# PSUM addressed as eight single banks and a new hand-written order, in a kernel of block-sorted attention followed by a gated MLP

## The chip, the core and the metric

The kernel runs on one core of a Trainium2 chip. The metric is the device time of one execution in microseconds (us), and the lower one is the better. The core has five engines with a queue of instructions each: TensorE (PE, with the weight loads PEld beside it), VectorE (DVE), ScalarE (ACT), GpSimd (POOL) and SyncE (SP). An engine takes its instructions strictly in the order in which they were written for it. DMAs are issued from the queues of POOL, SP and ACT, and run beside the engines.

## What is computed

Four batches go through two stages. The first sorts blocks softly: a small matrix `sort_net` is exponentiated and normalised five times, and the result P mixes the eight blocks of 96 tokens of K and of V; each block of Q then attends to its mixed block. The second is an MLP whose gate mixes tokens.

```python
def _attn_ref(q, k, v, sort_net):          # q, k, v: (4, 8, 768, 64); sort_net: (4, 8, 8, 8)
    P = sort_net
    for _ in range(5):
        P = P - np.max(P, axis=-1, keepdims=True)
        P = np.exp(P)
        P = P / (np.sum(P, axis=-1, keepdims=True) + 1e-09)
        P = P / (np.sum(P, axis=-2, keepdims=True) + 1e-09)
    k_sorted = np.einsum('bhij,bhjcd->bhicd', P, k_b).reshape(B, H, S, D)
    v_sorted = np.einsum('bhij,bhjcd->bhicd', P, v_b).reshape(B, H, S, D)
    scores = scale * np.matmul(q_b, k_sb.transpose(0, 1, 2, 4, 3))
    ...
    return np.matmul(attn, v_sb).reshape(B, H, S, D)

def _moe_ref(x, w_in, w_spatial, b_spatial, w_out):   # x: (4, 768, 512), d_ff 1024
    h = np.maximum(x @ w_in, 0.0)
    u, v = h[..., :512], h[..., 512:]
    v_n = (v - mu) / np.sqrt(var + 1e-06)
    v_s = np.einsum('ts,bsd->btd', w_spatial, v_n) + b_spatial[None, :, None]
    return (u * v_s) @ w_out
```

## The kernel before

The whole program is one string, `ORDER` (L18 to L52), which is read from left to right. Each word is a unit, and its parts after the colons are arguments: `KT:2:A:3:1` calls `u_KT` with PSUM tile 2, evacuation on ACT (D would be DVE), batch 3, head pair 1. A unit writes its matmuls, then the copy that takes the result out of PSUM, each to the end of its engine's queue. So the string sets the order on all engines at once, and no scheduler moves anything. Waits between engines are put in by the tile framework where one instruction needs another's result, or a buffer that another still uses.

The units that the prediction speaks of are these.

- At the start: `SK` (L233) is one of five normalisations, a chain of small DVE and ACT instructions. `QC` casts half of a q load, `MA` and `MB` make a mask, `DM` (L226) multiplies a block of zeros to keep PE occupied, and `PR` (L256) spreads the finished P over partitions. `P0` (L270) makes the mixing matrices `pd` of batch 0 on DVE from it, and `PD` (L282) those of the other batches on POOL.
- Attention: `QT` and `QQ` transpose one or two head pairs of q. `KT` and `VT` (L383) mix K and V with `pd`, transposed; `VB` turns V of batch 0 back into the buffer `vb`. For the other batches `VM` (L410) mixes V into the buffer `vm` and `VC` (L424) copies it from `vm` into `vb[b % 2]` by DMA, one DMA for each of the eight blocks. `SC` makes scores and their exponentials, `AT` (L483) multiplies them with `vb` and normalises into `x_sb`. `IV` (L222) writes the columns of ones of a `vb` or of `vm`.
- MLP: `XT`, `XX` and `XD` transpose `x_sb` (PE or DMA), `WW` and `WT` transpose w_spatial. `VP` (L551) makes v of one or two token tiles, `ST`, `LN` and `LA` normalise it, `UP` (L593) makes u. `SP` (L608) mixes tokens and adds the bias into one of three buffers `z` (`NZ` is 3). `GT` (L625) multiplies z by u, on POOL or DVE, and `OP` is the output product. `QP` and `QX` transpose q of batch 3 by DMA. `L` issues a load from POOL's queue and `OS` a store.
- Tail: `SH`, `GH`, `OH`, `OI`, `OJ` do the last batch's SP, GT and output in smaller pieces after a flag has been tested (`IF`).

PSUM has eight banks of 512 words in each partition. `ps_tile(n)` (L105) gives every unit a tile of two banks, and with n from 0 to 3 there are four such tiles; a unit that fills one bank occupies a pair all the same. The next unit with the same n waits until the tile has been evacuated.

Of the kernel before, what the change touches and what calls it, by code (L numbers as in the profile page):

```python
# [15 lines left out]


ORDER = """  # L18
IV:0 L:q:0:4:8 L:v:0:0:8 S0 LH:A:0 TB CO L:k:0:0:8 SK:0 BH ID MA SK:1 L:k:1:0:8 SK:2 MC DM:0:6:512 QC:A:0 DM:0:6:512
SK:3 SK:4 DM:0:6:512 DM:0:6:512 QC:A:1 QT:0:A:0:3 DM:1:6:512 MB QT:1:A:0:2 DM:2:3:512 QT:2:D:0:0 PR:3 P0:0:2 P0:2:4  # L20
L:v:1:0:8 P0:6:8 P0:4:6 VT:0:A:0:0 VT:1:D:0:1 PC:D QT:2:A:0:1 VB:0:D:0:0 L:q:1:0:8 PD:1:4:8 VB:1:D:0:1 L:wv VT:2:A:0:3
VT:3:D:0:2 KT:0:A:0:1 KT:1:D:0:0 KT:2:A:0:3 KT:3:D:0:2 SC:0:0:1:0 PD:2:0:4 SC:1:0:1:1 VB:2:D:0:2 SC:0:0:0:1 AT:3:0:1:0
SC:1:0:2:0 PD:1:0:4 AT:2:0:1:1 SC:0:0:3:0 VB:3:D:0:3 SC:1:0:0:0 AT:2:0:0:1 KT:0:A:1:1 AT:3:0:2:0 SC:1:0:2:1
XT:2:D:0:1:0 AT:0:0:3:0 SC:3:0:3:1 VM:1:A:1:1 AT:2:0:0:0 PD:2:4:8 VM:3:A:1:3 AT:0:0:2:1 VM:1:A:1:0 AT:2:0:3:1
VM:3:A:1:2 XX:0:D:0:0 L:wu L:v:2:0:8 L:wsb L:q:2:0:8 KT:1:A:1:0 KT:2:D:1:2 KT:3:A:1:3 PD:3:0:4 QT:0:D:1:2 IV:2
QQ:1:D:1:0 VC:1:0:4 QT:2:A:1:3 XT:3:D:0:1:2 SC:0:1:2:0 SC:1:1:2:1 SC:2:1:0:1 VP:3:D:0:3 VP:0:D:0:0:4 SC:1:1:3:0
SC:3:1:0:0 VP:2:A:0:5:2 ST:0:3 UP:1:A:0:0:0 VC:1:4:8 L:k:2:0:8 VP:0:A:0:1 ST:0:2 AT:3:1:2:0 SC:2:1:1:0 AT:1:1:3:0
UP:0:A:0:1:1 AT:3:1:1:0 AT:2:1:0:0 L:wsa UP:1:A:0:0:1 VM:0:D:2:1 VM:3:A:2:3 XX:2:A:1:0 AT:1:1:2:1 AT:0:1:0:1 BI ST:0:5
UP:3:A:0:1:0 ST:0:1 VM:1:A:2:2 VM:2:A:2:0 L:k:3:0:8 ST:0:0 PD:3:4:8 VP:0:D:1:0:1 SC:3:1:3:1 IV:1 ST:0:4 SC:1:1:1:1
UP:2:A:1:0:0 LN:0:0:6 AT:3:1:3:1 WW:0:D:4 AT:1:1:1:1 UP:2:A:1:1:0 L:v:3:0:8 LA:0:5 LA:0:1 KT:3:A:2:3 QQ:0:D:2:0 LA:0:3  # L30
L:q:3:0:8 KT:1:A:2:1 KT:2:A:2:0 QQ:3:D:2:2 VC:2:4:8 LA:0:4 KT:0:A:2:2 WW:1:D:0 LA:0:2 SC:2:2:0:1 SC:3:2:3:1 VP:0:D:1:2
XX:1:D:1:1 SC:2:2:1:1 LA:0:0 SC:3:2:2:1 WW:0:D:2 UP:1:A:1:1:1 AT:2:2:0:1 AT:3:2:3:1 SP:0:0:2 AT:1:2:2:1 AT:2:2:1:1
SP:3:0:3 GT:P:0:3 XD:2:1 VC:2:0:4:0:4:A ST:1:1 SC:0:2:0:0 SC:1:2:1:0 SP:2:0:0 SP:3:0:1 SC:0:2:2:0 ST:1:0 SC:1:2:3:0
L:wo UP:2:A:1:0:1 VM:3:A:3:0 ST:1:2 AT:0:2:2:0 VP:1:A:1:4 KT:2:A:3:1 KT:3:D:3:0 KT:0:A:3:3 KT:1:A:3:2 GT:P:0:1
GT:D:0:0 QP:D:3:2 VP:2:D:1:3:5 QP:D:3:3 QP:A:3:1 QP:D:3:0 ST:1:4 GT:P:0:2 ST:1:3 VM:3:A:3:2 OP:0:0:2:2 OE:A:0:2 ST:1:5
VM:1:A:3:3 QX:3:0:4 VP:3:A:2:3:5 VP:2:A:2:4 LN:1:0:6 VM:0:D:3:1 LA:1:4 AT:1:2:0:0 OP:3:0:0:2 LA:1:1 LA:1:0 LA:1:2
LA:1:3 OE:A:0:0 VC:3:4:8:0:4:A VC:3:0:4 LA:1:5 AT:2:2:3:0 OP:0:0:4:2 OE:A:0:4 AT:1:2:1:0 SP:3:1:3 GT:P:1:3 ST:2:5
SC:2:3:1:0 SC:1:3:0:1 XD:2:0 ST:2:3 SP:0:1:0 SC:3:3:3:0 SC:2:3:3:1 SP:1:1:2 AT:0:3:3:0 AT:3:3:0:1 SP:2:1:1 AT:1:3:1:0
GT:P:1:1 VP:0:A:2:0 VP:3:A:2:2 OS:0:0 AT:2:3:3:1 VP:0:D:2:1 ST:2:1 SC:1:3:0:0 GT:P:1:2 SC:3:3:2:1 UP:2:D:2:1:0
GT:P:1:0 ST:2:0 ST:2:2 SC:0:3:2:0 ST:2:4 SC:1:3:1:1 UP:3:A:2:0:1 UP:2:A:2:0:0 OP:0:1:2:2 LN:2:0:6 OE:A:1:2 LA:2:1  # L40
LA:2:3 LA:2:2 LA:2:0 LA:2:4 AT:1:3:2:1 AT:3:3:1:1 XD:3:1 UP:2:A:2:1:1 OP:0:1:0:2 AT:1:3:2:0 LA:2:5 AT:2:3:0:0
OP:3:1:4:2 CK SP:1:2:2 XD:3:0 SP:2:2:3 UP:1:A:3:1:1 SP:2:2:0 VP:1:D:3:3 OE:D:1:4 GT:D:2:0 OE:A:1:0 OS:1:2:0:2:A
GT:P:2:3 SP:0:2:1 VP:2:A:3:4:0 GT:P:2:1 ST:3:4 UP:1:A:3:0:1 ST:3:0 GT:P:2:2 CF:3 OS:1:0 VP:0:A:3:5 ST:3:3 ST:3:5
VP:2:A:3:2:1 ST:3:2 ST:3:1 LF LN:3:0:6 LA:3:5 LA:3:0 LA:3:2 LA:3:4 UP:1:A:3:0:0 OP:0:2:0:2 OP:3:2:2:2 OE:A:2:0
OS:0:4:0:2:A OP:2:2:4:2 UP:1:A:3:1:0 OE:D:2:2 OS:0:2:0:2:A OE:A:2:4 LA:3:1 LA:3:3 SH:0:3:2:0 SH:3:3:3:0 GH:P:3:3:0
SH:2:3:0:0 GH:D:3:2:0 SH:0:3:1:0 GH:P:3:0:0 SH:3:3:1:1 SH:2:3:2:1 OS:2:4 GH:P:3:1:0 SH:1:3:3:1 OS:2:0 GH:D:3:1:1
SH:3:3:0:1 OS:1:4 GH:D:3:3:1 OS:2:2 GH:P:3:0:1 GH:P:3:2:1 IF OH:0:3:2:0:512:0:4 OI:A:3:2:0:512 OH:1:3:3:0:512:0:4
OH:2:3:0:0:512:0:4 OI:D:3:0:0:512 OI:A:3:3:0:512 OH:0:3:1:0:512:0:4 OJ:3:2:0:512:S OJ:3:3:0:512:A OI:A:3:1:0:512
OJ:3:0:0:512:S OH:1:3:4:256:512:0:4 OI:D:3:4:256:512 OH:3:3:5:0:256:0:4 OI:D:3:5:0:256 OJ:3:1:0:512:S OJ:3:4:256:512:A
OH:2:3:5:256:512:0:4 OJ:3:5:0:256:A OI:D:3:5:256:512 OH:0:3:4:0:256:0:4 OI:D:3:4:0:256 OJ:3:5:256:512:S OJ:3:4:0:256:A  # L50
"""


# [12 lines left out]
def kernel(  # L66
# [159 lines left out]
    def u_DM(ps, n, w):  # L226
        t = ps_tile(ps)
        for _ in range(int(n)):
            nc.tensor.matmul(t[:, 0, 0:int(w)], lhsT=warm[:, 0:128], rhs=warm[:, 0:int(w)], start=True, stop=True)  # L229
# [26 lines left out]
    def u_PR(ps):  # L256
        pr = ps_tile(ps)[:, 0, 0:NB * BH].rearrange("p (i y) -> p i y", i=NB)
        for i in range(NB):
            nc.tensor.matmul(
                pr[:, i, :], lhsT=spread[:, (i % NI) * NB:(i % NI + 1) * NB].rearrange("p j t -> p (j t)"),  # L260
                rhs=p_t[:, (i // NI) * BH:(i // NI + 1) * BH], start=True, stop=True,
            )
# [568 lines left out]
```

## Time and profile before

| what | value |
|---|---|
| median of 3 runs | 155.5 us (155.46 to 155.74) |
| the profiled execution | 155.7 us, of which 153.9 us are the span from the first to the last instruction |
| PE busy | 146.7 us, 95% of the span, 1686 matmuls |
| DVE busy | 114.4 us, 74% |
| ACT busy | 80.5 us, 52% |
| POOL busy | 44.3 us, 29% |
| DMA | 24.36 MB in 30693 packets, mean 158 GB/s |

A row of the chain of waits reads: start, duration, engine, result and line. The chain is followed back from the last instruction: at each step to what released it, or to the instruction before it on its engine. A row of the groups reads: line, engine, operation, result and operands with shapes, count, then busy us and mean ns of one. A row of the windows gives for a stretch of the span the busy time of each engine, the number of instructions in brackets, the granted clock, the mean number of DMA shares and GB/s.

### The profile page before, as it was taken

Reading aid. Unit: us, or ns where it says so; the run is one execution under the profiler, and the core shown is the slowest. Engines: PE = TensorE matmul, PEld = TensorE weight load, DVE = VectorE, ACT = ScalarE, POOL = GpSimd, SP = SyncE. Lnnn points to the kernel's source line nnn. Section 1 sums busy time; section 2 is a strip of 40 time slices with the busy share of each in tenths; the row PEclk is TensorE's granted clock in tenths of the full one; section 3 lists DMA queues with packets and bytes.
Section 4 is the critical chain, followed back from the end, with each engine's and each line's share of the span. In section 5 each row is a group of like instructions: output and inputs, shape, how many; then the busy total and the mean of one; then the engine's idle time right before and its main releaser. Section 6 shows DMA issues by size and latency. Waiting matters only on the chain.

```text
span 153.9 us, 4047 instructions
## 1 busy us (share of the span) xinstructions
PE 146.7 (95%) x1686; PEld 95.7 (62%) x1686; DVE 114.4 (74%) x260; ACT 80.5 (52%) x114; POOL 44.3 (29%) x48
## 2 busy tenths in 40 slices
...
GB/s 101 253 204 204 204 204 205 209 203 226 248 212 209 258 238 206 200 111 103 140 4 146 102 222 190 1 0 4 0 104 101 259 18 0 71 69 351 339 175 238
DMA packets 30693, 24.36 MB, mean 158 GB/s; under 512 B 10384, under 2 KB 27792, under 8 KB 30672
## 3 DMA queue, kind: packets, MB, share of 16 engines
...
q8 instruction: 14, 0.23, 0.6%
...
HBM read 24.78 MB, written 6.29 MB: 202 GB/s over the span
## 4 chain that ended last, share of the span: by engine, by line
PE 82%; DVE 6%; DMA 5%; issue 1%; SPq 1%; POOL 1%; ACT 1%; DVEq 0%; POOLq 0%; ACTq 0%
PE ps L613 15%; PE ps L601 13%; PE ps L558 10%; PE ps L639 10%; PE ps L229 7%; PE ps L669 5%; DMA vb<-vm 5%; PE ps L492 4%; PE ps L689 3%; PE ps L446 3%; PE ps L387 3%; PE ps L414 3%; PE ps L318 2%; DVE x_sb L500 2%; DVE vb L117 2%; PE ps L548 1%
## 5 line engine op out<-in xcount | busy, mean ns | idle before, releaser
L630 POOL TENSOR_TENSOR gt<-z,u_sb 128x768 bf16<-128x768 f32 x10 | 16.2, 1640 | 62.7 <-ACT ex_all L451 35.3
L451 ACT ACTIVATE ex_all<-ps 96x768 bf16<-96x768 f32 x32 | 24.1, 804 | 14.3 <-PE ps L446 14.3
L613 PE MATMUL ps<-wspT,v_sb 128*128 128x384 bf16 x144 | 25.1, 326 | 0.0
L601 PE MATMUL ps<-xT,w_in_sb 128*128 128x384 bf16 x128 | 23.3, 326 | 0.0
L558 PE MATMUL ps<-w_in_sb,xT 128*128 128x512 bf16 x96 | 22.9, 379 | 0.0
L500 DVE TENSOR_TENSOR x_sb<-ps,rec_all 96x512 bf16<-96x512 f32 x32 | 22.0, 687 | 1.1
L121 ACT ACTIVATE u_sb<-ps 128x768 bf16<-128x768 f32 x15 | 12.1, 809 | 17.2 <-PE ps L601 16.8
L613 PEld LDWEIGHTS <-v_sb 128*128 128x128 bf16 x144 | 13.6, 98 | 8.7
L575 DVE BATCH_NORM_STATS2 stats<-v_sb 128x6 f32<-128x512 bf16 x24 | 16.2, 674 | 3.0 <-ACT v_sb L121 3.0
L619 DVE TENSOR_TENSOR z<-ps,b_bc 128x768 f32<-128x768 f32 x12 | 11.5, 955 | 7.9 <-PE ps L613 7.9
L639 PE MATMUL ps<-w_out_sb,gt 128*128 128x256 bf16 x144 | 16.9, 272 | 0.0
L601 PEld LDWEIGHTS <-w_in_sb 128*128 128x128 bf16 x128 | 11.8, 98 | 7.5
L115 ACT COPY o_sb<-ps 128x1024 f32<-128x1024 f32 (+1 forms) x10 | 8.8, 882 | 13.0 <-PE ps L689 8.4
L639 PEld LDWEIGHTS <-gt 128*128 128x128 bf16 x144 | 13.9, 98 | 2.0
L558 PEld LDWEIGHTS <-xT 128*128 128x128 bf16 x96 | 8.8, 97 | 9.3
L121 ACT ACTIVATE v_sb<-ps 128x512 bf16<-128x512 f32 (+1 forms) x10 | 7.6, 767 | 11.4 <-PE ps L558 11.3
L492 PE MATMUL ps<-vb,ex_all 96*128 96x65 bf16 x256 | 12.4, 193 | 0.7 <-DMA vb<-vm 0.5
L492 PEld LDWEIGHTS <-ex_all 96*128 96x128 bf16 x256 | 10.7, 97 | 3.4 <-issue 1.0
L229 PE MATMUL ps<-warm 128*128 128x512 bf16 x33 | 10.1, 450 | 1.4 <-DVE warm L203 1.3
L285 POOL TENSOR_TENSOR pd<-mask,prep_sb 128x512 bf16<-128x512 bf16 x6 | 6.5, 1093 | 15.0 <-DVE prep_sb L117 9.5
L587 DVE TENSOR_SCALAR v_sb<-v_sb,mv,rstd 128x512 bf16<-128x512 bf16 x24 | 8.7, 405 | 1.7 <-ACT rstd L582 1.7
L499 DVE RECIPROCAL rec_all<-ps 96x8 f32<-96x8 f32 x32 | 6.3, 196 | 3.9 <-PE ps L492 3.9
...
## 6 DMA issues: line engine op xcount, KB each, us to landing
...
vb<-vm SPq DMA_DIRECT2D x16, 99.0 KB, 6.2
...
```

Source lines behind the costliest of these rows:

```text
L121: nc.scalar.activation(out=out, in_=in_, func=AF.Relu)
L229: nc.tensor.matmul(t[:, 0, 0:int(w)], lhsT=warm[:, 0:128], rhs=warm[:, 0:int(w)], start=True, stop=True)
L451: nc.scalar.activation(out=e_tile(b, hp, ih).rearrange("p h (x g) -> p h x g", g=G), in_=t[0:BLK, :, 0:HW].rearrange("p h (g x) -> p h x g ...
L492: nc.tensor.matmul(t[:, hh, ii * VW:ii * VW + D + 1], lhsT=e[:, c:c + 128], rhs=vb[b % 2][:, ih * NI + ii, 2 * hp + hh, 0:D + 1], start=Tr ...
L500: nc.vector.tensor_mul(out=x_sb[:, hp].rearrange("p i (h d) -> p h i d", h=2), in0=tv[:, :, :, 0:D], in1=_raw_ap(rec, 0, [rec.ap[0], [NI, ...
L558: nc.tensor.matmul(t[:, x, :], lhsT=st["xT", b][:, n // 3, kc, (n % 3) * 128:(n % 3 + 1) * 128], rhs=w_in_sb[:, kc, DH:DFF], start=(kc == ...
L575: nc.vector.bn_stats(out=stats, in_=st["v_sb", b, n])
L601: nc.tensor.matmul(t[:, x, 0:HW], lhsT=w_in_sb[:, kc, mc * 128:(mc + 1) * 128], rhs=st["xT", b][:, ih, kc, :], start=(kc == 0), stop=(kc = ...
L613: nc.tensor.matmul(t[:, x, 0:HW], lhsT=st["v_sb", b, n][:, mc * 128:(mc + 1) * 128], rhs=wspT[:, 3 * x:3 * x + 3, n, :], start=(n == 0), s ...
L619: nc.vector.tensor_add(out=z.rearrange("p (x c) -> p x c", x=2), in0=t[:, :, 0:HW], in1=b_bc.rearrange("p (x c) -> p x c", x=2),)
L630: eng.tensor_mul(out=gt, in0=st["z", b, mc], in1=u)
L639: nc.tensor.matmul(t[:, x, c:c + w], lhsT=st["gt", b, mc][:, (n0 + x) * 128:(n0 + x + 1) * 128], rhs=w_out_sb[:, mc, c:c + w], start=(mc = ...
```

## The change

Three things change. Matmul, copy and DMA code of the units stays as it is.

- `ps_tile` cuts from one tile of eight banks. With n below 10 it gives the pair of banks 2n and 2n+1 as before; with n from 10 it gives the single bank n − 10. The units `QT`, `VB`, `XT`, `WT`, `VP` with one token tile, `SH`, `OH`, `DM`, `PR` and `CF` now take single banks.
- The whole string `ORDER` is new, from the first word to the last. Some work is also grouped in another way: `QQ` goes from 3 units to 1 and `QT` from 6 to 10; `XX` from 3 to 0 and `XT` from 2 to 8; `WW` from 3 to 2 and `WT` from 0 to 2; `VP` from 17 to 22 units for the same 24 token tiles. All 24 V copies are issued from SP's queue; before, 16 were SP's and 8 ACT's.
- The `DM` units write 23 products where they wrote 33.

```diff
 ORDER = """
-IV:0 L:q:0:4:8 L:v:0:0:8 S0 LH:A:0 TB CO L:k:0:0:8 SK:0 BH ID MA SK:1 L:k:1:0:8 SK:2 MC DM:0:6:512 QC:A:0 DM:0:6:512
...
+S0 CO DM:10:5:512 IV:0 LH:A:0 TB SK:0 DM:10:3:512 L:q:0:4:8 BH ID SK:1 SK:2 IV:2 QC:A:0 DM:10:4:512 QC:A:1 SK:3 MA
...
 """
...
     psum = ctx.enter_context(tc.tile_pool(name="psum", bufs=1, space=bass.MemoryType.PSUM))
 
+    banks = psum.tile([128, 8, 512], FP32, name="ps", tag="ps")
+
     def ps_tile(n, dt=FP32):
-        return psum.tile([128, 2, 512 if dt == FP32 else 1024], dt, name=f"ps{n}", tag=f"ps{n}")
+        n = int(n)
+        t = banks[:, 2 * n:2 * n + 2] if n < 10 else banks[:, n - 10:n - 9]
+        return t if dt == FP32 else t.bitcast(dt)
```

Six lines are added ahead of the units, so that the line of a unit in the changed kernel is its line before plus six.

The first place is ACT's queue at the start. `p_all` is the exponential of a normalisation, `q_in` a cast of q, `spread` the identity that `PR` uses. Before:

```order
L241 ACTIVATE p_all<-p_all 32x64 x3
L220 COPY spread<-ident 32x512
L115 CAST q_in<-q_109 128x768
L241 ACTIVATE p_all<-p_all 32x64 x2
L115 CAST q_in<-q_109 128x768
L115 COPY qT<-ps_197 128x768
```

And in the changed kernel:

```order
L247 ACTIVATE p_all<-p_all 32x64 x3
L121 CAST q_in<-q_117 128x768 x2
L247 ACTIVATE p_all<-p_all 32x64
L226 COPY spread<-ident 32x512
L247 ACTIVATE p_all<-p_all 32x64
L121 COPY qT<-ps 128x1536
```

Both casts of q stand ahead of the fourth exponential now, and the identity behind it.

The second place is POOL's queue from the mixing matrices on. The `MEMSET` of `vm` is `IV:2`, without which no V copy is complete. Before:

```order
L178 DMA w_in_sb<-in_moe_w_in_dram 128x4x512
L170 DMA v_in<-in_v_dram 128x8x384
L184 DMA ws_in<-in_moe_w_spatial_dram 128x3x768
L170 DMA q_in<-in_q_dram 128x8x384
L285 TENSOR_TENSOR pd<-mask_88,prep_sb 128x512
L224 MEMSET vm 128x48x2
```

In the changed kernel that `MEMSET` stands near the start:

```order
L230 MEMSET vb_97 96x64x2
L176 DMA q_in<-in_q_dram 128x4x384
masks.py:197 MEMSET ident 128x128
masks.py:199 ISA
masks.py:199 AFFINE_SELECT ident<-ident 128x128
L230 MEMSET vm 128x48x2
L176 DMA v_in<-in_v_dram 128x8x384
```

It has moved from behind a product of `pd` to the start of the program, ahead of the load of v.

The third place is the end of POOL's loads. The `MEMSET` of `vb` is `IV:1`. Before, it stood ahead of the loads of v and q of batch 3:

```order
L285 TENSOR_TENSOR pd<-mask_88,prep_sb 128x512
L224 MEMSET vb_97 96x64x2
L170 DMA v_in<-in_v_dram 128x8x384
L170 DMA q_in<-in_q_dram 128x8x384
L630 TENSOR_TENSOR gt<-z,u_sb 128x768
```

In the changed kernel, with the semaphores that each row waits for (DMAHW are those of DMAs issued by SP or ACT), it stands behind the last load and among the `GT` products:

```order
L636 TENSOR_TENSOR gt<-z,u_sb 128x768 [waits DVE_49]
L176 DMA k_in<-in_k_dram 128x8x384 [waits DMASW4_49,DMASW1_49,PE_49]
L230 MEMSET vb_98 96x64x2 [waits DMAHW6_49,DMAHW5_49,DMAHW7_49,DMAHW1_49,DMAHW0_49]
L636 TENSOR_TENSOR gt<-z,u_sb 128x768 [waits DVE_49,Activation_49]
L636 TENSOR_TENSOR gt<-z,u_sb 128x768
```

The `MEMSET` has moved past the first V copies of batch 3 and waits for them; on SP, the first of the four later copies of that batch waits for POOL in turn:

```order
L433 DMA vb_98<-vm 96x1x528 [waits DMAHW5_49,DVE_49,Activation_49]
L433 DMA vb_98<-vm 96x1x528 [waits DMAHW6_49]
L433 DMA vb_98<-vm 96x1x528 [waits DMAHW7_49]
L433 DMA vb_98<-vm 96x1x528 [waits DMAHW0_49]
L516 DMA_TRANSPOSE xT<-x_sb 128x16x96 [waits DMAHW1_49,DVE_49]
L660 DMA out_dram<-o_sb 128x2x512 [waits DMAHW2_49]
L433 DMA vb_98<-vm 96x1x528 [waits DMAHW3_49,PE_49,Pool_49]
```

On DVE the bias product that follows the last K evacuations of batch 3 (`SP:0:1:2`) waits for POOL, because its `z` is one that a `GT` has to give back:

```order
L123 CAST kt_all<-ps 128x768 [waits PE_49]
L123 CAST kt_all<-ps 128x768 [waits PE_49,Activation_49]
L625 TENSOR_TENSOR z<-ps,b_bc 128x768 [waits PE_49,Activation_49,Pool_49]
L505 RECIPROCAL rec_all<-ps 96x8 [waits PE_49]
L506 TENSOR_TENSOR x_sb<-ps,rec_all 96x2x4x64 [waits DVE_49]
```

The first of these rows evacuates `KT:1:D:3:1`, and the last two belong to `AT:0:3:2:0`, whose products use the PSUM tile of that `SP`.

More of the change, by code (lines that the diff above doesn't have):

```diff
@@ L18 @@
 ORDER = """
-IV:0 L:q:0:4:8 L:v:0:0:8 S0 LH:A:0 TB CO L:k:0:0:8 SK:0 BH ID MA SK:1 L:k:1:0:8 SK:2 MC DM:0:6:512 QC:A:0 DM:0:6:512
[L20 to L48, printed above, removed]
@@ L49 @@
-OJ:3:0:0:512:S OH:1:3:4:256:512:0:4 OI:D:3:4:256:512 OH:3:3:5:0:256:0:4 OI:D:3:5:0:256 OJ:3:1:0:512:S OJ:3:4:256:512:A
-OH:2:3:5:256:512:0:4 OJ:3:5:0:256:A OI:D:3:5:256:512 OH:0:3:4:0:256:0:4 OI:D:3:4:0:256 OJ:3:5:256:512:S OJ:3:4:0:256:A
+S0 CO DM:10:5:512 IV:0 LH:A:0 TB SK:0 DM:10:3:512 L:q:0:4:8 BH ID SK:1 SK:2 IV:2 QC:A:0 DM:10:4:512 QC:A:1 SK:3 MA
+L:v:0:0:8 MC SK:4 QQ:0:A:0:0 DM:12:5:512 DM:12:4:512 L:k:0:0:8 QT:12:D:0:3 PR:13 L:v:1:0:8 MB DM:10:2:512 P0:0:2
+P0:2:4 P0:4:6 P0:6:8 VT:2:A:0:0 PC:A VT:3:D:0:1 QT:12:A:0:2 VB:10:D:0:0 PD:1:0:4 VB:11:A:0:1 VT:2:D:0:3 L:k:1:0:8
@@ new lines @@
+VT:3:A:0:2 KT:1:D:0:2 KT:0:A:0:0 KT:2:D:0:1 PD:1:4:8 KT:3:A:0:3 L:q:1:0:8 SC:1:0:2:1 VB:10:D:0:2 VB:11:D:0:3 L:wv L:wu
+SC:2:0:3:0 SC:3:0:3:1 L:wsb AT:1:0:2:1 SC:0:0:1:0 L:wsa AT:2:0:3:0 SC:1:0:0:0 AT:3:0:3:1 VM:0:A:1:1 AT:2:0:1:0
+SC:1:0:1:1 XT:16:D:0:1:2 VM:0:A:1:2 AT:2:0:0:0 SC:3:0:0:1 AT:1:0:1:1 SC:0:0:2:0 KT:2:D:1:1 KT:3:A:1:0 AT:1:0:0:1
+VM:0:D:1:0 VM:2:A:1:3 XT:16:A:0:0:0 AT:1:0:2:0 XT:17:D:0:1:0 KT:2:A:1:3 KT:0:A:1:2 QT:16:D:1:3 QT:12:D:1:0 QT:13:A:1:2
+L:v:2:0:8 QT:14:D:1:1 PD:2:4:8 XT:15:D:0:0:2 SC:3:1:0:0 BI SC:0:1:3:0 VC:1:0:4 SC:1:1:2:0 L:q:2:0:8 VP:14:D:0:3
@@ new lines @@
+VP:3:A:0:0:2 ST:0:3 PD:3:4:8 ST:0:2 VP:0:A:0:1:5 ST:0:0 VP:16:D:0:4 PD:3:0:4 ST:0:4 SC:2:1:1:1 SC:1:1:1:0 UP:0:A:0:0:0
+ST:0:1 ST:0:5 L:k:2:0:8 UP:3:A:0:0:1 WW:2:A:4 AT:1:1:2:0 AT:0:1:0:0 LN:0:0:6 L:q:3:0:8 UP:3:A:0:1:0 LA:0:3 AT:1:1:3:0
+AT:2:1:1:0 LA:0:1 WW:0:A:2 UP:3:A:0:1:1 LA:0:4 XT:12:D:1:0:2 XT:13:D:1:0:0 VC:1:4:8 LA:0:2 SC:2:1:0:1 LA:0:0
+SC:0:1:2:1 SC:3:1:3:1 PD:2:0:4 WT:12:A:0 LA:0:5 WT:13:A:1 UP:2:D:1:1:0 VP:10:A:1:1 AT:3:1:1:1 VP:11:A:1:2 VM:2:D:2:1
+AT:1:1:3:1 VM:3:A:2:2 SP:0:0:2 AT:2:1:0:1 AT:3:1:2:1 SP:1:0:3 VM:0:A:2:3 UP:2:A:1:0:0 VM:3:A:2:0 SP:1:0:0 GT:P:0:3
@@ new lines @@
+GT:P:0:0 KT:0:A:2:1 QT:16:D:2:0 QT:17:D:2:1 KT:2:A:2:2 KT:1:D:2:0 QT:10:A:2:3 QT:11:D:2:2 KT:3:A:2:3 L:wo QP:D:3:1
+ST:1:2 SC:2:2:1:1 SC:1:2:0:1 XT:10:D:1:1:0 XT:11:A:1:1:2 SP:3:0:1 SC:2:2:3:1 SC:1:2:0:0 VP:11:A:1:0 L:v:3:0:8 VC:2:4:8
+ST:1:1 AT:3:2:1:1 AT:2:2:0:1 VP:10:A:1:4 SC:1:2:2:0 GT:D:0:2 VC:2:0:4:0:4 SC:3:2:2:1 VP:11:A:1:5 AT:2:2:3:1
+VP:10:D:1:3 SC:1:2:3:0 SC:3:2:1:0 ST:1:0 GT:P:0:1 ST:1:4 QP:A:3:2 ST:1:3 UP:2:A:1:0:1 OP:0:0:2:2 ST:1:5 AT:1:2:2:1
+OE:A:0:2 AT:3:2:3:0 OP:2:0:0:2 LN:1:0:6 LA:1:0 LA:1:5 LA:1:1 QP:A:3:3 OE:A:0:0 OP:0:0:4:2 OE:A:0:4 LA:1:4 LA:1:3
@@ new lines @@
+VM:1:A:3:3 VM:3:A:3:1 QP:A:3:0 LA:1:2 SP:2:1:0 XD:2:1 QX:3:0:4 VM:0:A:3:2 AT:1:2:0:0 SP:3:1:1 L:k:3:0:8 VM:2:D:3:0
+AT:0:2:1:0 SP:1:1:3 OS:0:2:0:2 UP:3:A:1:1:1 VC:3:0:4 AT:2:2:2:0 KT:0:A:3:0 IV:1 KT:1:D:3:1 XD:2:0 GT:P:1:3 KT:3:D:3:2
+GT:P:1:1 KT:2:A:3:3 SP:0:1:2 SC:1:3:2:0 SC:2:3:2:1 VP:16:A:2:5 AT:0:3:2:0 VP:17:D:2:3 SC:1:3:3:0 SC:2:3:0:1 OS:0:4:0:2
+ST:2:3 ST:2:5 SC:0:3:1:1 VP:16:D:2:4 VC:3:4:8:0:4 AT:1:3:3:0 VP:17:A:2:0 UP:2:A:2:1:1 AT:0:3:2:1 VP:16:D:2:2 ST:2:2
+SC:1:3:0:0 ST:2:0 GT:P:1:0 SC:2:3:1:0 SC:0:3:3:1 ST:2:4 VP:17:A:2:1 UP:1:A:2:1:0 ST:2:1 UP:2:A:2:0:0 GT:P:1:2 LN:2:0:6
```

11 lines of the change are left out of this document (added).

## The prediction

> **What bounds the kernel now.** I read the chain of waits first, by engine and then piece by piece, then the windows of ten microseconds, then the waits.
>
> ```profile
> PE 82%; DVE 6%; DMA 5%; issue 1%; SPq 1%; POOL 1%; ACT 1%; DVEq 0%; POOLq 0%; ACTq 0%
> ```
> ```profile
> 0.00:10.00 10.00, 8.40 (x37) 3.20 (x38) 5.88 (x31) 3.67 (x8) 6.20 (x13) 1.00 0.92 184
> ...
> 20.00:30.00 10.00, 9.77 (x202) 7.42 (x202) 9.40 (x21) 9.28 (x14) 5.83 (x7) 1.00 1.30 207
> 30.00:40.00 10.00, 9.80 (x141) 5.99 (x136) 6.38 (x10) 7.16 (x10) 5.46 (x7) 1.00 1.23 218
> 40.00:50.00 10.00, 9.33 (x112) 6.23 (x110) 7.49 (x18) 6.94 (x10) 2.04 (x3) 1.00 1.27 219
> 50.00:60.00 10.00, 10.00 (x193) 7.36 (x191) 9.69 (x20) 8.04 (x14) 0.00 (x0) 1.00 1.24 238
> ...
> 140.00:150.00 10.00, 10.00 (x66) 6.20 (x64) 6.20 (x13) 1.76 (x3) 5.21 (x5) 1.00 0.72 278
> ```
>
> The columns behind the colon are the length, then PE, PEld, DVE, ACT and POOL busy. PE is full from 50 us on; a gain can come only from the first 42 us or from less PE work, and a new wait behind them costs its full length. Three stretches lie ahead. The first:
>
> ```profile
> 1.28 2.76 PE ps L229 x6
> 4.04 0.04 issue
> 4.08 2.19 PE ps L229 x6
> 6.27 0.04 issue
> 6.31 1.47 PE ps L229 x6
> ...
> 11.94 0.77 PE ps L229 x3
> ...
> 13.79 0.42 DVE pd L273
> 14.21 0.14 issue
> 14.34 0.87 PE ps L387 x24
> ```
> ```profile
> 11.64 0.23 DVE L254 STREAM_TRANSPOSE p_t<-p 32x64 bf16<-32x64 bf16 x1
> ...
> 13.21 0.36 PE L259 MATMUL ps<-p_t,spread 32*128 32x32 bf16 x8
> ```
>
> P is ready at 11.64 + 0.23 = 11.87, yet `PR` (L259) begins at 13.21, because three filler products and a transpose of q stand ahead of it on PE. The filler also shows a clock that rises: the first six products take 2.76 us (0.46 each), the third six 1.47 us (0.245 each).
>
> From 15 to 33 us the chain runs mostly through DVE (9.40 of 10 us busy, ACT 9.28). From 30 us on it runs through POOL and SP:
>
> ```profile
> 30.54 1.08 POOL pd L285
> 31.62 0.14 POOL vm L224
> 31.76 0.02 issue
> 31.77 0.73 SPq L427
> ...
> 33.83 7.49 DMA vb<-vm
> 41.32 0.04 issue
> 41.36 0.31 PE ps L492 x5
> ```
> ```profile
> 26.45 2.89 ACT L115 CAST vm<-ps 128x768 bf16<-128x768 f32 x4
> ```
> ```profile
> 40.27 0.23 PE L492 MATMUL ps<-vb,ex_all 96*128 96x65 bf16 x2
> 40.65 0.19 PE L492 MATMUL ps<-vb,ex_all 96*128 96x65 bf16 x1
> 41.36 0.31 PE L492 MATMUL ps<-vb,ex_all 96*128 96x65 bf16 x5 [0.52 <-DMA vb<-vm]
> ```
>
> The vm copies end at 26.45 + 2.89 = 29.34, but SP issues the first V copy at 31.77, when POOL has written the ones of vm behind a product of `pd`. The first four land one by one up to 41.32, and five of the eight products of the first `AT` of batch 1 wait; from 40.27 + 0.23 to 41.36 PE does 0.19 us of work, so it loses some 0.7 to 0.9 us there. I take 0.8.
>
> **The change part by part.** *Ten products less.* They are 10 × 0.245 = 2.45 us of PE work, all of it in time in which PE would wait for P; by themselves they are worth nothing. What counts is what stands ahead of `PR`. In the new order the first 12 products end where the first 12 end now, near 6.27; `QQ` and 9 × 0.245 = 2.2 us of filler follow and end before P. P itself hardly moves: the mask's reduction leaves the second normalisation, where it lay on the DVE chain, and comes back in the fifth, and two casts stand ahead of the fourth exponential in place of one. I take 12.0 for P (0.1 later). Then come, on DVE, a copy of q that has now nothing to wait for (0.5), the mask and `P0`, so `P0` begins near 12.65 in place of 13.79 and `VT` near 13.2 in place of 14.34: **1.15 us earlier**. Up to 33 us the time is DVE's. Along the new order I count 17.5 us of DVE work from `VT` to the first `VP`, with the durations of before, where 17.9 stood; but ACT has 18.9 where it had 17.5, so the two engines are nearly level and the lead may shrink or grow on the way: 0.8 to 1.6 us. I keep 1.15.
>
> *The ones of vm* stand at POOL's start now, where nothing waits behind them but loads. SP can issue when the vm copies are done, near 29.3, 2.4 us earlier. The fourth copy would land at 29.3 + (33.83 − 31.77) + 7.49 = 38.9. PE comes to the first `AT` of batch 1 later than now: one `UP` and one `WW` more stand ahead of it (1.30 by the row below and, as an estimate, 0.67), and 1.15 is gained, so about 40.5 − 1.15 + 2.0 = 41.3. The wait of **0.8 us goes**; it comes back only if the copies land over 2.4 us later than reckoned.
>
> *Loads, all V copies on SP, PSUM as banks.* SP issues eight copies more, at 0.6 to 0.7 us each (the SPq rows), and is idle at those places. The K load of batch 1 now stands behind a product of `pd`; by the loads' rate in the windows (204 GB/s and more, 3.85 us for 786 KB) each load still lands 2 us or more before its use, so I cost them at nothing; a load that came late would cost its lateness in full. The single banks give PE more places to write into, which helps only where PE waits for an evacuation. The price stands on ACT: token tiles evacuated one by one cost more than in pairs.
>
> ```profile
> L121 ACT ACTIVATE v_sb<-ps 128x1024 bf16<-128x1024 f32 x4 | 4.1, 1023 | 6.6 <-PE ps L558 6.6
> ...
> L121 ACT ACTIVATE v_sb<-ps 128x512 bf16<-128x512 f32 x6 | 3.6, 596 | 4.8 <-PE ps L558 4.7
> ```
>
> Two singles take 2 × 0.596 = 1.19 where a pair takes 1.02, and five pairs are broken up: 0.9 us. With w_spatial's copies, which go from DVE to ACT, I count 5.8 us more on ACT, of some 80. ACT and DVE are both between 60 and 90% busy from 41 to 91 us, so a short wait of PE here and there is likely: bounds 0 and 1.5 (two waits for an evacuation of 0.8), **I take 0.5 lost**.
>
> *The ones of vb* (`IV:1`) are the part that I think costs. They stood far ahead of the V copies of batch 3; now POOL's `MEMSET` waits until the first four of these copies have landed, with `GT:P:1:3` behind it on POOL. The z of `SP:0:1:2` needs the buffer that this `GT` gives back, and `AT:0:3:2:0` on PE needs the PSUM pair of that `SP`. DVE stands still behind that z too. The rows of the chain's links:
>
> ```profile
> 84.85 0.96 DVE L117 CAST vm<-ps 128x768 bf16<-128x768 f32 x1 [1.14 <-PE ps L414]
> ```
> ```profile
> 85.96 2.78 SPq L427 DMA_DIRECT2D vb<-vm  x4
> ```
> ```profile
> vb<-vm SPq DMA_DIRECT2D x16, 99.0 KB, 6.2
> ...
> vb<-vm ACTq DMA_DIRECT2D x8, 99.0 KB, 3.0
> ```
> ```profile
> L630 POOL TENSOR_TENSOR gt<-z,u_sb 128x768 bf16<-128x768 f32 x10 | 16.2, 1640 | 62.7 <-ACT ex_all L451 35.3
> ...
> L619 DVE TENSOR_TENSOR z<-ps,b_bc 128x768 f32<-128x768 f32 x12 | 11.5, 955 | 7.9 <-PE ps L613 7.9
> ```
>
> From the end of `VM:2:D:3:0` on PE: the z before it and the vm copy on DVE 1.6 (0.65 left of 0.955, and 0.96), the start of the last of four issues 2.2, its landing 3.0 (the median of the copies of ACT's queue, all after 60 us, when few loads run), the memset 0.2, `GT` 1.64, z 0.96: about 9.6 us. PE's work up to `AT:0:3:2:0` in that time is two `AT`, two `SP`, an `UP`, four `KT`, two `SC` and one tile of `VP`:
>
> ```profile
> 42.30 1.30 PE ps L601 x8
> ...
> 57.66 0.34 PE ps L387 x12
> ...
> 88.80 0.24 PE ps L492 x8
> 89.04 1.95 PE ps L613 x12
> 90.99 0.45 PE ps L446 x16
> ...
> 100.65 0.86 PE ps L558 x4
> ```
>
> 2 × 0.24 + 2 × 1.95 + 1.30 + 4 × 0.34 + 0.45 + 0.86 = 8.35, and some 0.25 of turns between them: 8.6. **PE waits 1.0 us.** Bounds: 0 (the copies land 1 us sooner) and 4.2 (6.2 us to land, the median of SP's copies).
>
> *The tail* from the first `SH` on has the same units, with other banks: nothing.
>
> The sum: 155.7 − 1.15 − 0.8 + 0.5 + 1.0 = 155.25 for the profiled execution. The median of the runs is 0.2 below the profiled one: **155.0 us**.
>
> **The rivals.** *A, the late chain is covered.* If ACT or DVE lose a microsecond earlier on PE's account, or the copies land in 2 us, PE never meets that wait: 155.0 − 1.0 = **154.0**. For it: PE's way of 8.6 us is only a tenth shorter than the chain. Against: what delays PE also delays the vm copy at the chain's head.
>
> *B, the late chain is long (slower).* The place is the same, the price is the landing of the V copies. It decides from 3.5 us on, where the change has no gain left. With 4.4 us, half-way between the 3.0 and 6.2 of the rows, it is 155.0 + 1.4 = 156.4; with 6.2 it is 158.2. For it: the last K load is issued shortly before in the new order, behind SP's transpose of q, and the one landing above with loads beside it took 7.49 us. Against: in the new order this load has some 8 us of PE work ahead of the copies, two times its 3.85. I put it at **156.8**.
>
> *C, PE's clock.* The first 12 products rose from 0.46 to 0.245 each only with PE occupied without a break up to 9.3 us. With 12 products, a pause of a microsecond until q is cast, and waits for P, the rise may come late or be undone: `QQ`, 9 products and `QT` then take about twice as long (1.05, 2.2 and 0.53 us more), `VT` comes 2.6 us later than reckoned, and the transposes after it lose 0.4: **158.0**. For it: PE is busy in some 60% of the time from 6 to 12 us. Against: the products between 4.08 and 6.27 had sped up by then (2.19 for six), so 4 to 5 us of work sufficed. [...]
>
> *D, the middle.* ACT's 5.8 us more, in order, meet PE at more than two places between 41 and 91 us: four waits of 0.8 more than I took, less what is also covered later (1.0, since the wait at the late chain shrinks only if DVE is not late as well): **157.2**. For it: ACT was at 8.04 of 10 us between 50 and 60 us. Against: single banks let PE run ahead of a late evacuation.
>
> **How the numbers follow.** Two kernels can be told apart from about 0.2%, 0.3 us. My forecast has 0.38, with its own range 154.4 to 155.6 from the bounds of the lead and of the small waits. A has 0.17, B 0.24, C 0.07, D 0.14. Faster than 155.2: 0.6 of the forecast, all of A, a little of D: 0.42. Within 0.3 us: 0.3 of the forecast and a little of B and D: 0.14. Slower: 0.44, nearly all of B, C and D. The range that leaves out the far ends of A, B and C is 153.4 to 158.0.
>
> **What would show it.** Right: `PR` right behind P and the first `VT` near 13.2 us; the first V copy on SP near 29.3 and no wait of PE for `vb` near 41 us; near 85 us a POOL `MEMSET` that waits for DMA, a z of DVE that waits for POOL and one PE gap of about 1 us; PE busy lower by 2.5 us. Wrong: a first `VT` after 14 us or filler products of over 0.4 us after 7 us (C); no gap near 90 us (A), or one of over 2 us (B); many gaps of 0.3 to 0.8 us between 41 and 91 us with ACT as releaser (D); a K, V or weight load as releaser of PE, which I have excluded.

## The result, and the profile after

| | before | changed |
|---|---|---|
| median of 5 runs each | 155.5 us (155.45 to 155.74) | 154.98 us (154.75 to 155.29) |
| ratio, 95% interval | | 0.9961 (0.9946 to 0.9975) |
| the profiled execution | 155.7 us, span 153.9 | 155.29 us, span 153.5 (the slowest of the five) |

The change makes the kernel 0.4% faster, and the forecast was 155.0 us. The sum came out; not all of its terms did. The windows of the changed kernel (start and end, length, then PE, PEld, DVE, ACT, POOL busy):

```profile
0.00:10.00 10.00, 6.74 (x44) 2.93 (x45) 5.97 (x32) 4.63 (x10) 4.59 (x12) 1.00 0.94 186
20.00:30.00 10.00, 9.21 (x203) 7.28 (x203) 9.31 (x22) 9.17 (x14) 5.29 (x7) 1.00 1.29 204
30.00:40.00 10.00, 9.57 (x113) 5.37 (x108) 7.08 (x16) 7.43 (x10) 4.60 (x5) 1.00 1.17 229
40.00:50.00 10.00, 10.00 (x144) 7.49 (x143) 7.82 (x21) 8.98 (x13) 0.00 (x0) 1.00 1.28 230
...
90.00:100.00 10.00, 9.17 (x102) 5.10 (x103) 6.73 (x14) 5.94 (x9) 6.61 (x5) 1.00 0.60 146
140.00:150.00 10.00, 9.16 (x63) 5.83 (x61) 5.91 (x13) 1.76 (x3) 4.84 (x5) 1.00 0.45 169
```

PE is full from 40 us on now, ten microseconds earlier than before. But two stretches that were full have holes of 0.83 and 0.84 us: 90 to 100 and 140 to 150. The first of them in the kernel before:

```profile
90.00:100.00 10.00, 10.00 (x106) 5.99 (x104) 7.51 (x15) 4.28 (x6) 1.97 (x2) 1.00 0.43 124
```

The start of the changed kernel, as the timeline has it by engine:

```profile
11.40 0.23 DVE L260 STREAM_TRANSPOSE p_t<-p 32x64 bf16<-32x64 bf16 x1
11.57 0.51 DVE L123 COPY qT<-ps 128x768 bf16<-128x768 bf16 x1
11.69 0.35 PE L265 MATMUL ps<-p_t,spread 32*128 32x32 bf16 x8 [0.78 <-DVE p_t L260]
...
12.26 1.42 DVE L279 TENSOR_TENSOR pd<-mask,ps 128x256 bf16<-128x256 bf16 x4
...
12.74 0.86 PE L393 MATMUL ps<-pd,v_in 128*64 128x128 bf16 x24 [0.17 <-DVE pd L279]
```

PE now waits for P (0.78 us) instead of P for PE. The chain of waits of the changed kernel at the late V copies, and at the tail:

```profile
84.71 0.26 PE ps L498 x8
85.01 0.38 issue
85.39 0.96 DVE vm L123
...
86.41 0.61 SPq L433
...
87.71 3.03 DMA vb<-vm
...
90.81 0.61 issue
91.45 0.13 POOL vb L230
...
91.62 1.64 POOL gt L636
93.28 0.97 DVE z L625
...
94.29 0.40 PE ps L498 x8
...
136.22 7.80 PE ps L675 x48
144.02 0.84 issue
144.86 5.39 PE ps L695 x32
```

The first part is the chain that the prediction drew, link by link: the vm copy, SP's issues, landing (3.03 us), memset, `GT`, z, `AT`. The waits of the whole span (total us, times, longest) confirm its two ends:

```profile
POOL vb L230 <- DMA vb<-vm: 21.3, 1, 21.3
...
DVE z L625 <- POOL gt L636: 2.1, 1, 2.1
...
PE ps L498 <- DVE z L625: 0.8, 1, 0.8
```

The second part is new: 0.84 us of "issue" between the last `SH` (L675) and the first `OH` (L695) on PE, where PE waits for nothing that the chain shows. Before, the two followed without a hole:

```profile
137.65 7.80 PE ps L669 x48
145.45 5.21 PE ps L689 x32
```

Up to `SH` both kernels have the same PE work behind them but for ten filler products, so the time at which `SH` begins is a measure of the lead, which is how far the changed kernel is ahead: 137.65 − 136.22 = 1.43 us. At the first `OH` it is 145.45 − 144.86 = 0.59.

| moment | before | reckoned | changed |
|---|---|---|---|
| P ready | 11.87 | 12.0 | 11.63 |
| first `P0` | 13.79 | 12.65 | 12.26 |
| first `VT` | 14.34 | 13.2 | 12.74 |
| first V copy on SP | 31.77 | 29.3 | 28.80 |
| `SH` begins | 137.65 | 137.2 | 136.22 |
| `OH` begins | 145.45 | 145.0 | 144.86 |

"Reckoned" for the last two rows is the time before less the predicted lead of 1.15 + 0.8 − 0.5 − 1.0 = 0.45.

### The profile page after: what moved, and what is told of

Read it like the earlier page. It is cut to its first block, busy times and chain, and to the rows that moved or that the text cites. A ratio compares the mean times of both kernels' runs of the same rounds, so it can differ in the third digit from the quotient of the medians.

```text
span 153.5 us, 4093 instructions
## 1 busy us (share of the span) xinstructions
PE 142.8 (93%) x1676; PEld 94.5 (62%) x1676; DVE 114.7 (75%) x264; ACT 85.0 (55%) x122; POOL 42.5 (28%) x47
## 4 chain that ended last, share of the span: by engine, by line
PE 77%; DVE 11%; issue 3%; ACT 2%; DMA 2%; POOL 1%; SPq 1%; ACTq 0%; DVEq 0%; POOLq 0%
PE ps L564 13%; PE ps L607 13%; PE ps L619 13%; PE ps L645 10%; PE ps L675 5%; PE ps L498 5%; PE ps L452 4%; PE ps L695 4%; PE ps L393 3%; PE ps L420 3%; PE ps L528 2%; DMA vb<-vm 2%; PE ps L324 2%; DVE x_sb L506 2%; PE ps L411 1%
## 5 line engine op out<-in xcount | busy, mean ns | idle before, releaser
L636 POOL TENSOR_TENSOR gt<-z,u_sb 128x768 bf16<-128x768 f32 x9 | 14.6, 1637 | 49.6 <-DVE z L625 26.4
L564 PE MATMUL ps<-w_in_sb,xT 128*128 128x512 bf16 x96 | 23.4, 380 | 0.0
L127 ACT ACTIVATE v_sb<-ps 128x512 bf16<-128x512 f32 (+1 forms) x15 | 9.9, 657 | 15.9 <-DVE bad L722 8.7
L127 ACT ACTIVATE u_sb<-ps 128x768 bf16<-128x768 f32 x12 | 9.7, 810 | 10.3 <-PE ps L607 10.3
L498 PEld LDWEIGHTS <-ex_all 96*128 96x128 bf16 x256 | 10.7, 97 | 4.5 <-issue 1.6
L498 PE MATMUL ps<-vb,ex_all 96*128 96x65 bf16 x256 | 11.8, 193 | 1.0 <-DVE z L625 0.8
L688 POOL TENSOR_TENSOR gt<-z,u_sb 128x512 bf16<-128x512 f32 (+1 forms) x5 | 5.2, 1048 | 18.4 <-DVE z L681 18.4
L121 ACT CAST vm<-ps 128x768 bf16<-128x768 f32 x9 | 7.2, 808 | 4.9 <-PE ps L420 4.7
L452 PE MATMUL ps<-qT,kt_all 64*128 64x96 bf16 x256 | 8.8, 204 | 0.8 <-issue 0.4
## 6 DMA issues: line engine op xcount, KB each, us to landing
w_in_sb<-in_moe_w_in_dram POOLq DMA_DIRECT2D x2, 512.0 KB, 13.2
```

Source lines behind the costliest of these rows:

```text
L121: nc.scalar.copy(out=out, in_=in_)
L127: nc.scalar.activation(out=out, in_=in_, func=AF.Relu)
L452: nc.tensor.matmul(t[:, hh, 0:HW].rearrange("p (g x) -> p g x", g=G)[:, :, ii * TB:(ii + 1) * TB], lhsT=kT[rows, i * BLK:i * BLK + 128], r ...
L498: nc.tensor.matmul(t[:, hh, ii * VW:ii * VW + D + 1], lhsT=e[:, c:c + 128], rhs=vb[b % 2][:, ih * NI + ii, 2 * hp + hh, 0:D + 1], start=Tr ...
L564: nc.tensor.matmul(t[:, x, :], lhsT=st["xT", b][:, n // 3, kc, (n % 3) * 128:(n % 3 + 1) * 128], rhs=w_in_sb[:, kc, DH:DFF], start=(kc == ...
L636: eng.tensor_mul(out=gt, in0=st["z", b, mc], in1=u)
```

## The experiments

All times are medians, and every ratio is against runs of the kernel before that were timed beside the kernel in question. Kernels e1 to e4 were timed together.

**e1, the changed kernel again.**

> The changed kernel unaltered, as the yardstick of the runs beside it. If the 0.84 us in which PE waits at the branch into the tail belong to the program, PE's branch takes over 1 us again (1.76 us in the first profile, 0.39 us in the kernel before). If they were an accident of that execution, the branch takes some 0.4 us in this profile.

154.90 us (154.52 to 155.53, 11 runs), ratio 0.9959 (0.9943 to 0.9976). The branch into the tail, in the view of its line (count, duration in ns as minimum, median and maximum, start); first the kernel before, then the first profile of the changed kernel, then e1:

```profile
L797 PEldq COMPARE_BRANCH  x1: 392/392/392, 144.5 to 144.5; - x1
```
```profile
L803 PEldq COMPARE_BRANCH  x1: 1761/1761/1761, 143.0 to 143.0; - x1
```
```profile
L803 PEldq COMPARE_BRANCH  x1: 1421/1421/1421, 143.1 to 143.1; - x1
```

The long branch belongs to the program. The hole between `SH` and `OH` is 0.50 us in this profile, 0.34 less than in the first, as the branch is 0.34 shorter.

**e2, the ones of vb early.**

```diff
-... SK:2 IV:2 QC:A:0 ... VC:3:0:4 AT:2:2:2:0 KT:0:A:3:0 IV:1 KT:1:D:3:1 ...
+... SK:2 IV:2 IV:1 QC:A:0 ... VC:3:0:4 AT:2:2:2:0 KT:0:A:3:0 KT:1:D:3:1 ...
```

> Only the write of ones into the second vb (IV:1) moves from behind the first V copies of batch 3 to the start of POOL's queue. Theory (the late wait is POOL's, through GT and z): the 0.8 us gap of PE near 93.5 us goes, and the time falls by 0.8 to 1.2 us against the changed kernel, to some 154.0 us. Rival (the wait is only passed on, for instance to the V copies 4 to 7 or to the next z): the gap moves and the time stays within 0.3 us.

153.88 us (153.62 to 154.07), ratio 0.9889 (0.9872 to 0.9907): 1.02 us less than e1. POOL's `GT` products begin three microseconds earlier (91.62 in the changed kernel), waiting for an evacuation by ACT and for no DMA:

```profile
88.60 4.84 POOL L636 TENSOR_TENSOR gt<-z,u_sb 128x768 bf16<-128x768 f32 x3 [19.04 <-ACT u_sb L127]
```

and the chain from the last vm product to past `AT:0:3:2:0` is PE alone:

```profile
83.84 0.33 PE ps L420 x2
84.17 0.24 PE ps L498 x8
...
91.95 0.97 PE ps L564 x4
92.92 0.24 PE ps L498 x8
```

The wait was POOL's and is not passed on.

**e3, ten narrow products more.**

```diff
-... QC:A:0 DM:10:4:512 QC:A:1 ...
+... QC:A:0 DM:10:4:512 DM:10:10:64 QC:A:1 ...
```

> Only ten filler products of 64 columns are added at the start, in time in which PE waits for the cast of q; their results are read by nobody. Theory (PE's wait at the branch comes from where the last block of code before the branch is fetched, which 28 instructions fewer on PE moved right up to the branch): the fetch moves 20 instructions away from the branch, PE's branch falls back to some 0.4 us, and the time falls by 0.6 to 1.0 us against the changed kernel. Rival (the wait comes from the test of the flag, from the stores beside it or from chance): the branch keeps over 1 us and the time stays within 0.3 us.

154.09 us (153.82 to 154.32), ratio 0.9904 (0.9889 to 0.992): 0.81 us less than e1, from twenty instructions of work that nobody needs. The branch took

```profile
L803 PEldq COMPARE_BRANCH  x1: 741/741/741, 142.6 to 142.6; - x1
```

and `OH` follows `SH` without a hole. So the long branch is the cause of the hole. (The two profiles also differ ahead of it: `SH` begins at 135.82 in e3 and at 136.27 in e1, since the late wait is 0.6 us in the one and 1.4 in the other.) What makes it long is read from the packets by which code arrives; the trace marks them as instruction packets. One queue brings 14 blocks of 16 KB over the span, which I take for PE's, since 3372 of the 4047 instructions in the trace of the kernel before are PE's (1686 matmuls and as many weight loads). This is the queue's row (packets, MB, share) in the window from 137 to 139 us of the kernel before, then from 142 to 143 us of the changed one, then from 139.5 to 141 us of e3:

```profile
q8 instruction: 1, 0.02, 3.0%
```
```profile
q8 instruction: 1, 0.02, 6.7%
```
```profile
q8 instruction: 1, 0.02, 4.0%
```

The last block ahead of the branch, by the start of its packet, and the branch:

| kernel | block starts | branch starts | distance us | branch takes us |
|---|---|---|---|---|
| before | 137.52 | 144.47 | 6.95 | 0.392 |
| e3 | 140.97 | 142.64 | 1.67 | 0.741 |
| e1 | 142.18 | 143.09 | 0.91 | 1.421 |
| changed | 142.38 | 143.04 | 0.66 | 1.761 |
| e2 | 141.06 | 141.50 | 0.44 | 1.881 |

The nearer the block, the longer the branch. The seven other kernels fit (distance, branch): e10 0.63, 1.862; e5 0.76, 1.762; e4 1.68, 0.661; e7 2.21, 0.482; e9 3.02, 0.481; e8 4.06, 0.482; e6 6.16, 0.392. Wherever the block started less than 2 us ahead, the branch ended 2.3 to 2.5 us after the block's start, and in the rows of the table the block always started ahead of the branch. That the branch waits for this block is my reading; why it would is not shown.

The long branch has a second price: the output products `OH` take 5.39 us behind it (changed, e1, e2, e5, e10) and 5.21 where it is short (before, e3, e4). With the hole that makes 0.84 + 0.18 = 1.02 us in the first profile of the changed kernel and 0.50 + 0.18 = 0.68 in e1's.

**e4, both.** The two diffs of e2 and e3.

> Both edits, the early IV:1 and the ten narrow products. If both losses are independent and on the path, the time falls by 1.4 to 2.2 us against the changed kernel, to about 153.1 us. If one of them only covers the other, it falls by no more than the larger one.

153.16 us (153.02 to 153.68), ratio 0.9852 (0.9833 to 0.9871): 1.74 less than e1, near the 1.02 + 0.81 of the two. Both losses lay on the path, and the ten narrow products are worth 153.88 − 153.16 = 0.72 us also without the late wait.

**e5, the ones of vm behind a product of pd.**

```diff
-... SK:2 IV:2 QC:A:0 ... PD:2:4:8 XT:15:D:0:0:2 ...
+... SK:2 QC:A:0 ... PD:2:4:8 IV:2 XT:15:D:0:0:2 ...
```

> The changed kernel with the write of ones into vm (IV:2) put back behind a product of pd on POOL, as in the kernel before. Theory (that move took away the wait of PE for the first V copies of batch 1): the first V copy on SP is issued later, PE waits for vb near 41 us again, and the time rises by 0.5 to 1.2 us. Rival (in the new order PE comes late enough to these copies anyway): no wait near 41 us and no change of over 0.3 us.

154.92 us (154.53 to 155.43), ratio 0.9952 (0.9938 to 0.9966): no change against e1. But the edit did not delay anything: POOL wrote the ones at 23.35 us, and SP issued its first V copy at 28.79. So it could not tell the two theories apart, hence e10.

**e10, the ones of vm behind three products of pd.**

```diff
-... SK:2 IV:2 QC:A:0 ... PD:2:4:8 XT:15:D:0:0:2 ... ST:0:3 PD:3:4:8 ST:0:2 ... PD:3:0:4 ST:0:4 ...
+... SK:2 QC:A:0 ... PD:2:4:8 PD:3:4:8 PD:3:0:4 IV:2 XT:15:D:0:0:2 ... ST:0:3 ST:0:2 ... ST:0:4 ...
```

> The changed kernel with the write of ones into vm behind all three products of pd on POOL that stand near 30 us, so that SP's first V copy can be issued only near 31.8 us, as in the kernel before (in e5 it stood behind one product of pd, which was done at 23.4 us, and nothing waited for it). The first four copies then land near 41.9 us. Theory of the prediction (the early ones are what took the wait away): PE waits near 41 us, and the time rises by 0.5 to 1.0 us against the changed kernel. Rival (the new order, which brings PE to the first AT of batch 1 at 41.6 us, hides the late copies): PE waits at most 0.3 us and the time stays within 0.3 us.

154.84 us (154.49 to 155.31, 12 runs), ratio 0.9954 (0.994 to 0.9969): no change. SP's queue, and PE at the first `AT` of batch 1 (L498):

```profile
31.87 5.95 SPq L433 DMA_DIRECT2D vb<-vm  x8
```
```profile
40.21 0.83 PE L541 MATMUL ps<-ident,ws_in 128*128 128x128 bf16 x12
40.88 0.65 PE L498 MATMUL ps<-vb,ex_all 96*128 96x65 bf16 x16
41.37 1.47 PE L607 MATMUL ps<-xT,w_in_sb 128*128 128x384 bf16 x8
```

The copies leave as late as before the change, PE has no wait, and it comes to this `AT` at the same time as in e1, where they leave early (41.05 us in both chains). The rival holds: with the new order the early ones are not needed. It is close, though. PE begins this `AT` 0.6 us later than in the kernel before (40.88 against 40.27), and the last packet of the first four copies ends 0.45 us earlier (39.71 against 40.16); the two together are little more than the 0.7 to 0.9 us that PE lost before.

**e6, the kernel before with the ones of vm early.**

```diff
-... BH ID MA ... QT:0:D:1:2 IV:2 QQ:1:D:1:0 ...
+... BH ID IV:2 MA ... QT:0:D:1:2 QQ:1:D:1:0 ...
```

> The kernel before with that one unit (IV:2) moved to the start of POOL's queue and nothing else. Theory: SP's first V copy is issued near 29.4 us instead of 31.8, the gap of PE near 41 us goes, and the time falls by 0.7 to 0.9 us, to some 154.7 us. Rival (the copies then run against the loads and land no earlier): within 0.3 us.

154.72 us (154.38 to 155.29) against 155.66, ratio 0.9942 (0.9923 to 0.9961): 0.94 less. SP's first copy was issued at 29.97, and PE's chain there has no hole:

```profile
40.11 0.86 PE ps L558 x4
40.97 0.24 PE ps L492 x8
```

In the old order the early ones are worth what the prediction put on them; in the new order something else had already paid.

**e7, the kernel before with ten filler products fewer.**

```diff
-... DM:0:6:512 DM:0:6:512 QC:A:1 QT:0:A:0:3 DM:1:6:512 MB QT:1:A:0:2 DM:2:3:512 QT:2:D:0:0 PR:3 ...
+... DM:0:6:512 DM:0:5:512 QC:A:1 QT:0:A:0:3 MB QT:1:A:0:2 QT:2:D:0:0 PR:3 ...
```

> The kernel before with ten filler products fewer (one of the fourth group, and all nine ahead of and behind the second transpose of q), 23 as in the changed kernel; nothing else. Theory: PR and P0 follow P at once, VT starts 0.8 to 1.2 us earlier, but the DVE chain to 33 us keeps only a part of it: the time falls by 0.2 to 1.0 us. Rival (the wait for the V copies of batch 1, which start with POOL, takes it all back): within 0.2 us.

154.11 us, ratio 0.9894 (0.9879 to 0.9909), a median over two groups: four executions with a granted clock of 1.0 over the span took 153.75 to 154.13 us, two with 0.987 took 155.47 and 155.52. The profile is of the latter. Its windows (the granted clock is the third number from the end):

```profile
9.80:13.20 3.40, 1.70 (x57) 1.55 (x54) 2.87 (x13) 2.36 (x4) 0.00 (x0) 1.00 1.31 203
13.25:16.60 3.35, 3.35 (x49) 2.98 (x45) 2.47 (x6) 1.60 (x2) 1.13 (x2) 0.50 1.31 203
16.65:20.00 3.35, 3.29 (x96) 2.90 (x92) 3.17 (x4) 2.85 (x5) 1.63 (x2) 1.00 1.32 205
```

Without the nine products ahead of `PR`, PE is busy for 1.70 of the 3.4 us up to 13.2. Then half the clock was granted from 13.2 to 16.6 us. The other execution at 0.987 has no trace, but the same time, so I take it for the same. What decides it is not shown: four executions had the same work and kept the clock, and so did the changed kernel with a little less work in as long a stretch:

```profile
4.00:7.40 3.40, 1.62 (x17) 0.65 (x16) 2.42 (x12) 1.54 (x4) 1.53 (x2) 1.00 1.26 249
```

Where it held, the gain is 155.66 − 154.05 = 1.6 us (154.05 is the middle of the four), more than either theory gave.

**e8, the kernel before with PSUM as banks.** `ps_tile` as in the change, `ORDER` as before.

> The kernel before with PSUM as one tile of eight banks, and its own order, which takes pairs alone. Theory: the same waits in the same places, within 0.2 us of the kernel before. Rival (one tile for all makes the framework put in other waits): a difference of over 0.3 us.

155.19 us (154.88 to 155.34), ratio 0.997 (0.9959 to 0.9981): 0.47 less, where the theory gave nothing. The semaphores of PE's rows tell why. In the kernel before, 48 rows of PE wait for the semaphore that PE alone raises; the first three are the filler products that start at 4.08, 6.31 and 7.82 us, each the first of a new `DM` unit, which takes the tile that the unit before it wrote. In e8 and in the changed kernel there is no such wait. I read these waits as PE running empty at each change of tile before it goes on: from 4 to 12 us it is busy for 7.62 us in the kernel before and for all 8.00 in e8. The chain of the kernel before at the start, and that of e8:

```profile
9.43 0.53 PE ps L318 x12
9.95 1.42 PE ps L229 x6
...
12.75 0.54 PE ps L318 x12
```
```profile
9.02 0.46 PE ps L322 x12
9.47 1.40 PE ps L233 x6
...
11.33 0.75 PE ps L233 x3
12.08 0.47 PE ps L322 x12
```

The last transpose ahead of `PR` ends at 12.08 + 0.47 = 12.55 in place of 12.75 + 0.54 = 13.29: 0.7 us, all of it ahead of `P0`. e8 has no single banks, only pairs taken from one tile, so it is the one tile for all that helps.

**e9, the old order with three edits.** PSUM as banks, the ones of vm early, and `DM:2:3:512` taken out.

> The kernel before in its own order, with three edits: PSUM as eight banks (e8), the ones of vm written at POOL's start (e6), and the three filler products (DM:2:3:512) that stood on PE behind P taken out; the other 30 stay. If the three gains are separate, the time falls by 0.47 for the banks, 0.94 for the ones and, by the 0.6 us in which PE and DVE come earlier to P0, by 0.6: to about 153.6 us, with a granted clock of 1.0 in all executions, since PE has no pause ahead of P. Rival (the start's gains are worth nothing when the V copies of batch 1 set the time, or the other way round): no lower than 154.5 us.

153.06 us (153.02 to 153.22), ratio 0.9833 (0.9812 to 0.9854), with a granted clock of 0.997 to 1.0. That is 2.65 us less than the kernel before, where the three gains were expected to add up to 2.0; which of them is worth more here was not tried. The fastest kernel of this study, beside e4, has the old order.

## Why the prediction was right, and where it was not

**The start: the mechanism was right, its size 0.45 us too small.** Reckoned 1.15, measured 14.34 − 12.74 = 1.60. P came 0.2 earlier and not 0.1 later. The mask's reduction delayed the second normalisation by some 0.2 before; at its new place (9.53 to 9.89 us) it falls into DVE's wait for the fifth exponential and costs nothing, and the two casts were done at 7.81, when the fourth exponential needed ACT at 7.87. The copy of q and the mask took 0.6 us to `P0`, about as reckoned. What failed is the sentence that the banks help only where PE waits for an evacuation. Taken from one tile, they also take away PE's waits for itself, worth 0.47 us in the old order (e8). That ten products are worth nothing by themselves was misleading too: all of them stood ahead of `PR`, nine of them close ahead of it, and taking them out of the old order alone gave 1.6 us while the clock held (e7). The two gains probably overlap, since both end where P sets the time; no run has them alone together. PE's busy time fell by 3.9 us (146.7 to 142.8) and not by 2.5; 0.9 of the difference is the first 12 products, which took 4.08 us in place of 4.95, with the clock at full earlier in that execution: the trace's record of the granted clock begins, at 1.0, at 3.99 us in place of 5.57, and the products take 606 to 631 ns each ahead of it, one across it 471, and 379 to 380 behind it (before, 584 to 634, 511 and 376 to 380).

**The V copies of batch 1: the wait went, as forecast, but not by the move that I named.** The step that failed reads "SP can issue when the vm copies are done, near 29.3". It can, and did at 28.80, but it need not: with the copies at 31.87 the time is the same (e10). The new order has one `UP` and one `WW` more ahead of the first `AT` of batch 1, which I had in the sum as a mere shift. That PE comes later and that the copies land sooner hide the late ones between them (e10); what each gives was not tried apart. In the old order the early ones are needed, and bring 0.94 (e6).

**The middle: too pessimistic.** From `VT` to `SH` the lead went from 1.60 to 1.43. With 0.8 won at the V copies and 0.83 lost at the late chain, some 0.14 remains for everything else, where I had put 0.5. The windows show PE full from 40 to 90 us, so ACT's greater load met no path there. The split between the middle and the late chain belongs to this one execution, as the next paragraph shows. How much the single banks give, and how much the order, was not tried apart either.

**The late chain: right, in place, links and size.** From the end of `VM:2:D:3:0` at 84.71 to `AT:0:3:2:0` at 94.29 it measured 9.6 us, as reckoned, with 8.75 of PE work (reckoned 8.6) and a gap of 0.83 (reckoned 1.0). Taken out, it was worth 1.02 (e2). The landing of 3.0, on which the slower rival turned, was 3.03. The gap is not the same in every execution: in e1's profile it is 1.42 us. There PE comes to this place 0.54 us earlier, mostly because a hole of 0.43 us at 31.51 us in the first profile is missing, and yet the `AT` begins at 94.34, no earlier than 94.29. In these two executions a lead ahead of 84 us is lost here again.

**The tail: wrong.** The step that failed reads "the same units, with other banks: nothing". It overlooked that the length of the program ahead of a branch is itself changed: 28 instructions fewer on PE. 1.02 us were lost there in the first profile, 0.84 in the hole and 0.18 behind it, and 0.68 in e1's. Ten narrow products bring 0.81 back (e3), or 0.72 without the late wait (e4 against e2).

**The sum.** Of the predicted 0.45 of lead at `SH`, 1.43 came: 0.45 more from the start, 0.36 from the middle and 0.17 from the late chain. The tail took 0.84 of it, and the slower output stage behind the long branch another 0.18. So 0.4 us of the span remained, as forecast: three errors on one side and one on the other, of like size. That the time was right to 0.02 us is luck; the account was not right.

**The rivals.** A (late chain covered) and B (late chain long) did not happen. In B's price, half-way between 3.0 and 6.2 is 4.6 us and not 4.4, which makes 156.6 in place of 156.4. C, the clock, did not happen in the changed kernel, whose clock was 0.996 to 1.0 in all executions, but e7 shows that it was a real danger, at a price of 155.5 − 154.05 = 1.45 us. D did not happen: PE is full from 40 to 90 us.
